# Forming the output projection weight gradients of layers 3 and 2 inside the attention backwards of layers 3 and 1

## The chip, the cores and the metric

The kernel runs on one core of a Trainium2 chip. The core has five engines, each with its own instruction stream: TensorE (PE in the profile; its weight loads have a row of their own, PEld), VectorE (DVE), ScalarE (ACT), GpSimd (POOL) and SyncE (SP), which here issues every DMA transfer from one queue. The metric is the device time of one execution in microseconds; lower is better.

## The reference

Four residual layers with the same shapes, A, B, A, B; layers 0 and 2 share the weights of A, layers 1 and 3 those of B. T = 2048 rows, D = 640, 32 heads of 20. All tensors are bf16. Only the middle of each layer differs:

```
layernorm(x):  (x - mean) / sqrt(var + 1e-5)
A:  qkv = ln @ wqkv;  phi(t) = where(t > 0, t + 1, exp(t)) + 1e-6
    o = phi(q) (phi(k)^T v) / (phi(q) . sum_s phi(k) + 1e-6)      # no mask, whole sequence
B:  qkv = ln @ wqkv
    o = softmax(q k^T * 20**-0.5, where 0 <= i - j < 256) v       # sliding window
x = x + o @ wo                                                    # after each layer
```

The kernel returns the output and, for a given gradient `grad_out`, the gradients of x, A_wqkv, A_wo, B_wqkv and B_wo (`jax.vjp`). The weight gradients are sums over the two layers that share a weight. With `o[l]` the attention output, `g[l]` the gradient behind layer l, `hn[l]` the normalised input and `dqkv[l]` the gradient of qkv,

```
dWo_B = o[3]^T g[3] + o[1]^T g[1]         dWo_A = o[2]^T g[2] + o[0]^T g[0]        (640 x 640)
dW_B  = hn[3]^T dqkv[3] + hn[1]^T dqkv[1] dW_A  = hn[2]^T dqkv[2] + hn[0]^T dqkv[0] (640 x 1920)
```

A change here concerns when these four sums are formed and by which instructions.

## The kernel before, in words

Rows are handled in 16 tiles of 128. `passes` (L1350 onwards) runs the stages one after the other:

1. `forward`, to about 660 us: all four layers; `o`, `hn` and other tensors of each layer go to DRAM.
2. `core(st, 3, ...)`, the attention backward of layer 3, about 664 to 1082 us.
3. The linear backward of layer 2 (`plan_linear`), to about 1259 us.
4. `core(st, 1, ...)`, the attention backward of layer 1, about 1259 to 1666 us.
5. The linear backward of layer 0, in which the products of `weight_jobs` fill the gaps on PE, to about 1968 us.
6. What is left of `weight_jobs`, to the end.

**Order.** For PE, DVE, ACT and GpSimd the instructions run in the order in which this program issues them (`manual_schedule`). The DMA order on SP is chosen by the framework's scheduler. There is one queue on SP; a transfer that has to wait for its data holds everything behind it. The semaphores of the transfers go round in a set of eight, so that each transfer also waits for the one issued eight before it. `PLACES` (L39) holds positions of pieces of work in the visits, found beforehand.

**The core.** `core` (L1288) makes 192 visits and 6 more to drain: 8 chunks of two row tiles, and in each chunk 4 groups of heads (`qr`) of 6 visits. One `core_visit` (L690) works on several visits at a time, with a lag of 3, 4 and 6: it issues the score products `s` and the products `dp`, the exponential `e<-s` on ACT (L719), the product `ds<-dp,e` on DVE (L723), the masks on GpSimd (L734, L738), then the transposes of an older `ds` into a PSUM tile `flip` (L745) with its copy `dsT` (ACT L750, or DVE), a piece of the surrounding row work (`piece`: among it the dense products that share the PSUM pool), and the products `acc` of a still older visit (`core_acc`). Visits 0 to 23 (chunk 0) have tiles of 128 x 512, later ones 128 x 1024. From visit 48 on, the flip of some visits is made by DMA (`by_dma`, L673). The PSUM pool `st.ps` has two buffers under the tag "m", used by `flip`, `dense` and others; `s` and `dp` have one buffer each. The score products read slabs (`slabT`, `slabqT`, `slabqs`, `slabks`) that are loaded a group of six visits ahead.

Ahead of a `flip`, `warm` (L174 to L177) issues `thin` transposes of the identity matrix into unused columns of the same PSUM tile. Nothing reads their result. In visits 0 to 23 of each core there are `WARM[0]` = 8 of them, in 24 to 47 `WARM[1]` = 5, later 0 to 5 by `PLACES["th"]`; visits 0 to 3 have no flip and so none.

`hooks` (filled in `passes`, run in `core` at visit 0.75 k) hold the loads of transposed weights in the first visits of the core of layer 3: `turned` issues a DMA transpose (`WTB`, `WoTA`), and two of the results go back to DRAM (`WTAt`, `WoTBt`).

**The weight products.** `weight_jobs` (L1134) is a generator. It forms the four matrices in the order dWo_B, dW_B, dWo_A, dW_A. For each, blocks of w columns (240 for W, 160 for Wo; 480 and 320 when `W.wide`) and five row blocks m: one chain of 2 x 16 products into one PSUM bank `wg`, over both layers, then one eviction `wr<-wg` (ACT L1211 or DVE L1213) and one store. The left operand `lhs` (one layer's `o` or `hn`, 2.6 MB) comes from pools `wl` (2 buffers), `wl3` (1) and later `wl4` (2); `rhs` from two halves of a big tile, issued at m = 1 of the block before. In the linear backward, `fill(us)` pulls products until a credit is used up: 1.0 a slot after slot 24 of the rest of the core, 0.8 a slot of `plan_linear`; each product counts w/2400. Between the first matrix and the second, while lhs buffers are short (`W.tight`), the generator gives `yield 8.0`, which uses up ten slots. `fill(1e9)` at the end runs all that is left. The output tiles `wr` have 5 buffers in the linear stage and 4 of 480 columns behind it.

```
for n in range(48):
    thin[n] = self.WARM[n // 24]
```

Of the kernel before, what the change touches and what calls it, by code (L numbers as in the profile page):

```python
# [11 lines left out]
ALU = mybir.AluOpType  # L12
# [43 lines left out]
class Kern:  # L56
    def __init__(self, ctx, tc, x0, A_w, A_wo, B_w, B_wo, grad, outs):
# [19 lines left out]
        self.x2 = d("x2", [T, D])  # L77
        self.WTA, self.WoTB = d("WTAt", [P, NF * D]), d("WoTBt", [P, DT * D])
# [598 lines left out]
    WARM = (8, 5)  # L677
    TAIL = 5

# [10 lines left out]
    def core_visit(self, st, l, u, piece, on_act, thin):  # L690
# [443 lines left out]
    def weight_jobs(self, W):  # L1134

        nc = self.nc
        n = 2 * TT
        E = 4

        def lhs(arr):  # L1140
            t = W.lhs.pop(0).tile([P, TT, D], BF, name="lhs")
# [4 lines left out]
        def operand():  # L1146
            W.turn += 1
            if not W.wide:
                return W.big[:, W.turn % 2]
            if W.late is None:  # L1150
                W.late = W.wq2.tile([P, n, 480], BF, name="rhs2")
                W.turn = 1
            if W.turn % 2:
                return W.late
            return W.big.rearrange("p a n w -> p (a n w)").rearrange("p (n w) -> p n w", n=n)

        def rhs(arrs, c0, w):
            t = operand()
            for i, ar in enumerate(arrs):
                for a in range(0, TT, 8):  # L1160
                    self.dma(t[:, i * TT + a:i * TT + a + 8, 0:w], ar[a * P:(a + 8) * P, c0:c0 + w].rearrange("(t p) f -> p t f", p=P))
            return t

        def first(L, R, w):

            ls = [W.lhs.pop(0).tile([P, TT, D], BF, name="lhs") for _ in range(2)]
            r = operand()
            for i in range(2):
                for a in range(0, TT, 8):
                    self.dma(r[:, i * TT + a:i * TT + a + 8, 0:w], R[i][a * P:(a + 8) * P, 0:w].rearrange("(t p) f -> p t f", p=P))  # L1170
                    for b in range(a, a + 8, E):
                        self.dma(ls[i][:, b:b + E, :], L[i][b * P:(b + E) * P, :].rearrange("(t p) f -> p t f", p=P))
            return ls, r
        mats = []
        for kind, layers, names in (("B", (3, 1), ("Wo", "W")), ("A", (2, 0), ("Wo", "W"))):
            for mat in names:
                L, R, out, w, full = ((self.hn, self.dq, self.dW[kind], 240, QT) if mat == "W"
                                      else (self.o, self.gs, self.dWo[kind], 160, D))
                mats.append(([L[k] for k in layers], [R[k] for k in layers], out, w, full))

        def after(i, c0, w):
            c0 += w
            if c0 >= mats[i][4]:
                i, c0 = i + 1, 0
            if i == len(mats):
                return None
            return i, c0, mats[i][3] * (2 if W.wide and c0 + 2 * mats[i][3] <= mats[i][4] else 1)
        job, nxt = (0, 0, mats[0][3]), None
        while job is not None:
            i0, c0, w = job  # L1190
            L, R, out = mats[i0][:3]
            if nxt is None:
                nxt = first(L, R, w)
                yield 0.0
            ls, r = nxt
            for m in range(DT):
                if m == 1:
                    job = after(i0, c0, w)
                    if job is not None:
                        nxt = ls, rhs(mats[job[0]][1], job[1], job[2])  # L1200
                if m == 2 and job is not None and job[1] == 0:
                    L2 = mats[job[0]][0]
                    nxt = [lhs(L2[0]), None if W.tight else lhs(L2[1])], nxt[1]
                ps = W.ps.tile([P, 512], F32, name="wg")
                for i in range(n):
                    self.mm(ps[:, 0:w], ls[i // TT][:, i % TT, m * P:(m + 1) * P], r[:, i, 0:w], i == 0, i == n - 1)
                    if i < n - 1:
                        yield w / 2400.0
                o = W.out()
                if m % 2:  # L1210
# [3 lines left out]
                self.dma(out[m * P:(m + 1) * P, c0:c0 + w], o[:, 0:w])  # L1214
                yield w / 2400.0
            if nxt[0][1] is None:
                nxt[0][1] = lhs(L2[1])
                yield 8.0
# [69 lines left out]
    def core(self, st, l, g_out, B, hooks):  # L1288
# [17 lines left out]
        thin = [PLACES["th"][n % 24] for n in range(nv)]  # L1306
        for n in range(48):
            thin[n] = self.WARM[n // 24]
        on_act = [PLACES["xx"][n % 24] for n in range(nv)]
        n = 0  # L1310
        with ExitStack() as es:
# [3 lines left out]
            for c in range(NC):  # L1315
                for qr in range(4):
                    S = B.slabs.pop(0)
                    for i, u in enumerate(self.core_visits(st, l, S, c, qr, dq)):
# [12 lines left out]
                        self.core_visit(st, l, u, slots[n], on_act[n], thin[n])  # L1331
# [18 lines left out]
    def passes(self):  # L1350
# [6 lines left out]
        with ExitStack() as rest:  # L1357
# [17 lines left out]
            left3 = self.core(st, 3, self.gs[2], st.core, hooks)  # L1375
# [170 lines left out]
```

## Time and profile before

| what | value |
|---|---|
| time, median of 3 runs | 2187.86 us (2182.36 to 2193.05) |
| profiled execution: span, first to last instruction | 2185.5 us; no time beside the span is given for it |
| PE busy (matmul) | 2023.2 us, 93% |
| PE weight loads | 1564.4 us, 72% |
| DVE / ACT / GpSimd busy | 1338.7 / 1364.0 / 1040.7 us |
| mean granted clock of PE | 0.970 |
| identity transposes of L177 into `flip` | 764 |
| weight products `wg<-rhs,lhs` | 2880: 640 x 160 wide, 1280 x 240, 320 x 320, 640 x 480 |
| DMA | 426.92 MB, 708455 packets, mean 195 GB/s |

The visits of the two cores, by the start of their exponential: layer 3 visit 0 at 664.2, visit 10 at 683.3, visit 24 at 708.5, visit 48 at 759.6; layer 1 visit 0 at 1259.5, visit 4 at 1267.1, visit 24 at 1299.6, visit 48 at 1350.0.

How to read the profile: busy times of engines overlap, so they say where time could go and not what bounds it. The row PEclk tells what clock PE was granted, in tenths of full speed, in 40 slices of the span. A group line names the source line (L142 is the helper that issues every product), the engine, the operation and what it writes and reads. A bracket such as [4.69 <-DMA slabqT<-T] behind an instruction is the idle time of its engine before it, and what ended it.

### The profile page before, as it was taken

To read this page: it belongs to the slowest core of one execution; us is meant where nothing else is said; L and a number is where in the kernel's file an instruction comes from. 1 tells how busy PE (TensorE), PEld (TensorE's weight loads), DVE (VectorE), ACT (ScalarE), POOL (GpSimd) and SP (SyncE) were. 2 spreads that over 40 slices of the span, in tenths; PEclk is the share of its full clock that TensorE was granted. 3 is DMA by queue.
4 is the path that set the end of the run, shared out by engine and by line. 5 is a ranking of instruction groups with operands and counts; after the bars stand their busy time and mean duration, and the time that the engine had idled before them with its cause. 6 is when DMAs were issued, how large, how long until landed. Compare 5 with 4: busy or idle time off the path is not lost. (4 is left out here: it accounts for less than half of the span.)

```text
span 2185.5 us, 76656 instructions
## 1 busy us (share of the span) xinstructions
PE 2023.2 (93%) x32575; PEld 1564.4 (72%) x32575; DVE 1338.7 (61%) x2710; ACT 1364.0 (62%) x1907; POOL 1040.7 (48%) x1663
## 2 busy tenths in 40 slices
PE   7989998899988999999979989999998999999999
PEld 5667776577766877777758768777776888888644
DVE  6788886888844777777738747777776233320000
ACT  5468886388876888888737679888886133330000
POOL 2046665166665577777533456777764212220000
PEclk9999999999998999999889999999999999999999
DMA  7498985689888299998889922899998899988650
GB/s 258 149 224 225 227 206 145 158 218 209 226 223 211 69 177 188 188 188 176 164 263 255 234 82 74 185 196 188 187 196 186 265 309 241 276 202 252 210 163 21
DMA packets 708455, 426.92 MB, mean 195 GB/s; under 512 B 434320, under 2 KB 689040, under 8 KB 707728
## 3 DMA queue, kind: packets, MB, share of 16 engines
q1 hardware_dynamic: 708112, 422.03, 78.7%
q8 instruction: 254, 4.16, 0.8%
q14 instruction: 89, 0.73, 0.1%
HBM read 191.07 MB, written 141.43 MB: 152 GB/s over the span
## 5 line engine op out<-in xcount | busy, mean ns | idle before, releaser
L723 DVE TENSOR_TENSOR ds<-dp,e 128x1024 bf16<-128x1024 f32 (+1 forms) x384 | 443.9, 1156 | 166.0 <-PE s L142 80.5
L719 ACT ACTIVATE e<-s 128x1024 bf16<-128x1024 f32 (+1 forms) x384 | 380.1, 990 | 90.4 <-PE s L142 85.9
L387 ACT ACTIVATE eT<-sT 128x2048 bf16<-128x2048 f32 x180 | 338.0, 1878 | 96.5 <-PE sT L142 88.5
L142 PE MATMUL wg<-rhs,lhs 128*128 128x240 bf16 (+3 forms) x2880 | 374.2, 287 | 7.7 <-DMA lhs<-o 6.8
L142 PEld LDWEIGHTS <-lhs 128*128 128x128 bf16 x2880 | 262.6, 99 | 98.9 <-DMA lhs<-o 8.4
L738 POOL TENSOR_SCALAR_AFFINE_SELECT e<-e 128x256 bf16<-128x256 bf16 x512 | 201.6, 409 | 174.4 <-ACT e L719 143.8
L142 PEld LDWEIGHTS <-dqT 128*128 128x128 bf16 x1920 | 169.9, 98 | 66.7 <-issue 9.1
L395 POOL TENSOR_SCALAR_AFFINE_SELECT eT<-eT 128x512 bf16<-128x512 bf16 x256 | 164.7, 647 | 102.3 <-ACT eT L387 102.3
L750 ACT COPY dsT<-flip 128x1024 bf16<-128x1024 bf16 (+1 forms) x200 | 192.2, 961 | 12.4 <-PE flip L745 11.2
L142 PE MATMUL acc<-slabqs,ds 128*128 128x20 bf16 x2880 | 194.3, 172 | 0.6 <-ACT dq L805 0.5
L142 PE MATMUL acc<-ds,e 128*128 128x20 bf16 x2880 | 192.2, 171 | 0.0
L142 PE MATMUL dp<-slabT,dT 32*128 32x128 bf16 (+1 forms) x1952 | 154.1, 246 | 38.4 <-DVE ds L723 32.1
L142 PEld LDWEIGHTS <-ds 128*128 128x128 bf16 x2880 | 176.1, 96 | 10.9 <-issue 6.8
L1211 ACT CAST wr<-wg 128x240 bf16<-128x240 f32 (+3 forms) x36 | 14.3, 396 | 249.8 <-PE wg L142 249.8
L734 POOL TENSOR_SCALAR_AFFINE_SELECT e<-e 128x512 bf16<-128x512 bf16 x224 | 142.7, 637 | 55.6 <-ACT e L719 53.2
L142 PEld LDWEIGHTS <-e 128*128 128x128 bf16 x2880 | 164.1, 96 | 5.7 <-issue 0.5
L1213 DVE CAST wr<-wg 128x240 bf16<-128x240 f32 (+3 forms) x54 | 24.5, 453 | 231.3 <-PE wg L142 231.3
L142 PE MATMUL dense<-WTA,dqT 128*128 128x320 bf16 x960 | 163.5, 302 | 2.0 <-DMA dqT<-dqa 1.7
L1106 POOL TENSOR_TENSOR dh<-dh,lg 128x640 f32<-128x640 f32 x32 | 46.0, 1439 | 245.4 <-DVE s L1103 245.4
L142 PE MATMUL dense<-WB,hnT 128*128 128x320 bf16 x960 | 162.0, 303 | 0.4 <-DVE s L510 0.2
L142 PE MATMUL s<-slabT,slabqT 32*128 32x128 bf16 (+1 forms) x1952 | 148.4, 247 | 10.7 <-ACT e L719 5.2
L142 PE MATMUL dense<-WTB,dqT 128*128 128x320 bf16 x960 | 156.1, 301 | 1.1 <-DMA dqT<-dq 0.7
(175 smaller groups left out, 4445.4 us busy)
## 6 DMA issues: line engine op xcount, KB each, us to landing
T<-T SPq DMA_DIRECT2D x96, 256.0 KB, 3.3
s<-s SPq DMA_DIRECT2D x32, 512.0 KB, 3.7
slabT<-T SPq DMA_DIRECT2D x64, 256.0 KB, 3.9
dqkv<-dq SPq DMA_DIRECT2D x16, 960.0 KB, 5.9
dqkv<-dqa SPq DMA_DIRECT2D x32, 480.0 KB, 4.9
rhs<-dqkv SPq DMA_DIRECT2D x32, 480.0 KB, 5.9
rhs<-dqkv SPq DMA_DIRECT2D x16, 960.0 KB, 7.1
hn<-hn SPq DMA_DIRECT2D x64, 160.0 KB, 2.7
```

Of the source, the lines that this page charges most:

```text
L142: return self.nc.tensor.matmul(out, lhsT=lhsT, rhs=rhs, start=start, stop=stop, skip_group_check=True, **kw)
L387: nc.scalar.activation(e, s, ACT.Exp)
L395: nc.gpsimd.affine_select(out=e, in_=e, compare_op=ALU.is_ge, fill=0.0, base=0, pattern=[[0, 4], [1, P]], channel_multiplier=-1)
L719: nc.scalar.activation(u.e[:, :, 0:w], s[:, :, 0:w], ACT.Exp)
L723: nc.vector.tensor_tensor(out=d.ds[:, :, 0:w], in0=d.dp[:, :, 0:w], in1=d.e[:, :, 0:w], op=ALU.mult)
L734: nc.gpsimd.affine_select(out=v, in_=v, pattern=[[0, 4], [1 if far else -1, P]], **kw)
L738: nc.gpsimd.affine_select(out=v, in_=v, pattern=[[0, 2], [1 if far else -1, P]], **kw)
L750: nc.scalar.copy(v(f.dsT), v(ps))
L1106: nc.gpsimd.tensor_tensor(out=x["dh"], in0=x["dh"], in1=L["g"][:, i, :], op=ALU.add)
L1211: nc.scalar.copy(o[:, 0:w], ps[:, 0:w])
L1213: nc.vector.tensor_copy(o[:, 0:w], ps[:, 0:w])
```

## The change

Three parts belong together.

- **Early blocks.** `early_weights` forms o[3]^T g[3] in the core of layer 3, and o[2]^T g[2] in the core of layer 1, as 25 blocks of 128 x 128 each: 16 products 128 wide in a PSUM tile of tag "m" (`wgp`), one copy to an f32 tile by DVE, one store of 64 KB into a new DRAM tensor (`pw`). The left operand is 8 loads of 320 KB (`wgl`) into buffers of the pool `st.sp` that are used for other tiles later; the right operand is five column blocks of 512 KB (`wgr`, rows of 256 bytes), loaded two ahead. A block runs in `core_visit` ahead of the flip, in visits 10 to 46 of layer 3 (10 + 38i//25) and 4 to 46 of layer 1 (4 + 44i//25). In layer 3 the loads begin in `hooks[10]`, visit 7; in layer 1 ahead of the core.
- **Idle transposes.** From the first block on, `thin` is 0 in visits below 48, with or without a block. Those that stay are in visits 4 to 9 of layer 3 (8 each) and beyond visit 48. The whole kernel has 252 in place of 764.
- **The weight products.** `weight_jobs` is rewritten. The order is dW_B (both layers), dWo_B (layer 1 alone), dW_A (both), dWo_A (layer 0 alone). The Wo blocks are 320 wide with chains of 16, and DVE adds the partial sum, loaded back as f32 (`pt`, 3 buffers), while it evicts. The products are 2400: 1600 x 240, 320 x 320 and 480 x 480 (dW_A goes in blocks of 240, 480, 480, 480 and 240 columns); the pools of `lhs` shrink (no `wl4`), the output tiles are 2 of 320 columns in the linear stage, and the rest of `yield 8.0` is gone: while a left operand has no buffer, the generator gives `yield 1.0`.

On SP the change adds 84 transfers (1375 to 1459). In the core of layer 3 the scheduler now puts `wgr` and the eight `wgl` behind the third transpose of `WTB` from A, ahead of the next `slabqT`; the three transposes of `WTB` from B, one queue entry behind each other before, now come one by one behind the slabs of chunk 1; the load of `gb` and `WoTA` come later too. In layer 2's linear backward the eight `wgl` of the core of layer 1 are issued near its start. The rhs of the first block of `weight_jobs` goes ahead of all its lhs.

The diff, without the removed lines of `weight_jobs` (they stand above):

```diff
+        self.pw = {(k, nm): d(f"p{nm}{k}", [P, DT * w], F32) for k in "AB" for nm, w in (("Wo", D), ("W", QT))}
...
-    WARM = (8, 5)
+    WARM = 8
     TAIL = 5
+
+    def early_weights(self, st, la, dst):
+
+        w = 128
+        L, R = [], {}
+
+        def left():
+            for i, tag in enumerate(("hnb", "gc", "oa", "pqb", "gn", "gn", "dn", "dn")):
+                t = st.sp.tile([P, 2, D], BF, name="wgl", tag=tag, bufs=2 if i > 3 else 1)
+                self.dma(t, self.pair(self.o[la], i))
+                L.append(t)
+
+        def right(c):
+            R[c] = st.sp.tile([P, TT, w], BF, name="wgr", tag="dqT", bufs=3)
+            self.dma(R[c], self.gs[la][:, c * w:(c + 1) * w].rearrange("(t p) f -> p t f", p=P))
+
+        def block(c, m):
+            ps = st.ps.tile([P, 512], F32, name="wgp", tag="m")
+            for k in range(TT):
+                self.mm(ps[:, 0:w], L[k // 2][:, k % 2, m * P:(m + 1) * P], R[c][:, k, :], k == 0, k == TT - 1)
+            o = st.sf.tile([P, D], F32, name="wgo", tag="f")
+            self.nc.vector.tensor_copy(o[:, 0:w], ps[:, 0:w])
+            self.dma(dst[:, m * D + c * w:m * D + (c + 1) * w], o[:, 0:w])
+            if m == 0 and c + 2 < D // w:
+                right(c + 2)
+        return left, right, [lambda c=c, m=m: block(c, m) for c in range(D // w) for m in range(DT)]
...
+        if extra is not None:
+            extra()
         if f is not None and not f.by_dma:
...
         E = 4
...
+        def lhs(arr, pool):
+            t = pool.tile([P, TT, D], BF, name="lhs")
             for a in range(0, TT, E):
                 self.dma(t[:, a:a + E, :], arr[a * P:(a + E) * P, :].rearrange("(t p) f -> p t f", p=P))
             return t
...
+        def operand(n, w):
             W.turn += 1
...
+            if W.wide and W.late is None:
+                W.late = W.wq2.tile([P, 2 * TT * 480], BF, name="rhs2")
+                W.turn = 0
+            t = W.big[:, W.turn % 2] if not W.wide else W.big.rearrange("p a n -> p (a n)") if W.turn % 2 else W.late
+            return t[:, 0:n * w].rearrange("p (n w) -> p n w", n=n)
         def rhs(arrs, c0, w):
...
+            t = operand(len(arrs) * TT, w)
             for i, ar in enumerate(arrs):
                 for a in range(0, TT, 8):
...
+                    self.dma(t[:, i * TT + a:i * TT + a + 8, :], ar[a * P:(a + 8) * P, c0:c0 + w].rearrange("(t p) f -> p t f", p=P))
             return t
...
+        def sums():
+            for m in mats:
+                for c0 in range(0, D, 320):
+                    for j in range(DT):
+                        if m["mode"] == "add":
+                            yield part(m, c0, j, 320)
+        def part(m, c0, j, w):
+            t = W.out.tile([P, 320], F32, name="pt", bufs=3)
+            self.dma(t, m["part"][:, j * D + c0:j * D + c0 + w])
+            return t
+        def mat(mode, kind, nm, layers, c0=0, c1=None):
+            R, out, full = (self.dq, self.dW, QT) if nm == "W" else (self.gs, self.dWo, D)
+            return dict(mode=mode, L=[(nm, k) for k in layers], R=[R[k] for k in layers], out=out[kind], full=full, c0=c0, c1=c1 or full,
+                        part=self.pw[kind, nm], ls=[])
+        mats = [mat("all", "B", "W", (3, 1)), mat("add", "B", "Wo", (1,)), mat("all", "A", "W", (2, 0)), mat("add", "A", "Wo", (0,))]
+        want, at = [], {}
+        def pump():
+            while want and (W.lhs or want[0][1] in at):
+                m, arr = want.pop(0)
+                if arr not in at:
+                    at[arr] = lhs((self.hn if arr[0] == "W" else self.o)[arr[1]], W.lhs.pop(0))
+                m["ls"].append(at[arr])
+        def ask(i):
+            if i < len(mats):
+                want.extend((mats[i], k) for k in mats[i]["L"])
+                pump()
+        def blocks():
+            for i, m in enumerate(mats):
+                c0 = m["c0"]
+                while c0 < m["c1"]:
+                    w = 320 if len(m["R"]) == 1 else 240
+                    if W.wide and len(m["R"]) > 1 and c0 + 2 * w <= m["c1"]:
+                        w *= 2
+                    yield i, m, c0, w
+                    c0 += w
+        todo = blocks()
+        more, pt = sums(), []
+        i, m, c0, w = next(todo)
+        r = rhs(m["R"], c0, w)
+        nxt = (None, None, 0, 0)
+        ask(0)
+        yield 0.0
+        while m is not None:
+            pump()
+            while len(m["ls"]) < len(m["L"]):
+                yield 1.0
+                pump()
+            if c0 == m["c0"]:
+                for k in [k for k in at if k not in m["L"]]:
+                    del at[k]
+                ask(i + 1)
+            n = len(m["R"]) * TT
+            for j in range(DT):
+                pump()
+                if j == 1:
+                    nxt = next(todo, (None, None, 0, 0))
+                    if nxt[1] is not None:
+                        r2 = rhs(nxt[1]["R"], nxt[2], nxt[3])
+                if m["mode"] == "add" or nxt[1] is not None and nxt[1]["mode"] == "add" and j > 2:
+                    pt.append(next(more, None))
+                add = pt.pop(0) if m["mode"] == "add" else None
                 ps = W.ps.tile([P, 512], F32, name="wg")
...
+                for k in range(n):
+                    self.mm(ps[:, 0:w], m["ls"][k // TT][:, k % TT, j * P:(j + 1) * P], r[:, k, :], k == 0, k == n - 1)
+                    if k < n - 1:
                         yield w / 2400.0
...
+                o = W.out.tile([P, W.most], BF, name="wr")
+                if add is not None:
+                    nc.vector.tensor_tensor(out=o[:, 0:w], in0=ps[:, 0:w], in1=add, op=ALU.add)
+                elif j % 2:
                     nc.scalar.copy(o[:, 0:w], ps[:, 0:w])
                 else:
                     nc.vector.tensor_copy(o[:, 0:w], ps[:, 0:w])
...
+                self.dma(m["out"][j * P:(j + 1) * P, c0:c0 + w], o[:, 0:w])
                 yield w / 2400.0
...
+            (i, m, c0, w), r = nxt, r2
...
-            thin[n] = self.WARM[n // 24]
+            thin[n] = self.WARM if n < min(extra) else 0
...
+            work = {}
+
+            def begin_early(la, kind):
+                work["left"], work["right"], work["blocks"] = self.early_weights(st, la, self.pw[kind, "Wo"])
+                work["right"](0)
+                work["left"]()
+                work["right"](1)
+            h8 = hooks[10]
+            hooks[10] = lambda: (h8(), begin_early(3, "B"))
+            left3 = self.core(st, 3, self.gs[2], st.core, hooks, [(10 + i * 38 // 25, lambda i=i: work["blocks"][i]()) for i in range(25)])
...
+            begin_early(2, "A")
+            left1 = self.core(st, 1, self.gs[0], B, [f or (lambda: None) for f in hooks], [(4 + i * 44 // 25, lambda i=i: work["blocks"][i]()) for i in range(25)])
...
-            W.big, W.turn, W.wide, W.late = self.pool(rest, "wq", 1).tile([P, 2, 2 * TT, 240], BF, name="rhs"), 0, False, None
-            wo = self.pool(rest, "wo", 5)
+            W.big, W.turn, W.wide, W.late = self.pool(rest, "wq", 1).tile([P, 2, TT * 480], BF, name="rhs"), 0, False, None
+            W.out, W.most = self.pool(rest, "wo", 2), 320
             st.ex = self.pool(psl, "ex", 1)
-            W.lhs, W.tight = [wl, wl], True
-            W.out = lambda: wo.tile([P, 240], BF, name="wr")
+            W.lhs = [wl, wl]
...
-            wl4 = self.pool(rest, "wl", 2)
-            W.lhs += [wl4, wl4, wl, wl3]
-            W.tight, W.wide = False, True
-            W.wq2, wo2 = self.pool(rest, "wq2", 1), self.pool(rest, "wo2", 4)
-            W.out = lambda: wo2.tile([P, 480], BF, name="wr")
+            W.lhs += [wl, wl3]
+            W.wide, W.wq2 = True, self.pool(rest, "wq2", 1)
+            W.out, W.most = self.pool(rest, "wo2", 4), 480
             fill(1e9)
```

More of the change, by code (lines that the diff above doesn't have):

```diff
@@ L1174, in weight_jobs @@
[L1174 to L1203, printed above, removed]
+        def sums():
[4 more added lines that the diff above has]
+                            yield part(m, c0, j, 320)
@@ L1286, in core_loads, with core @@
         return S
-    def core(self, st, l, g_out, B, hooks):
+    def core(self, st, l, g_out, B, hooks, early):
         NC = TT // 2
@@ L1330, in core @@
                             dq[c] = dqp.tile([P, 2, QT], BF, name="dq")
-                        self.core_visit(st, l, u, slots[n], on_act[n], thin[n])
+                        self.core_visit(st, l, u, slots[n], on_act[n], thin[n], extra.get(n))
                         n += 1
@@ L1418, in passes @@
             self.core_buffers(st, B)
-            left1 = self.core(st, 1, self.gs[0], B, [f or (lambda: None) for f in hooks])
+            begin_early(2, "A")
+            left1 = self.core(st, 1, self.gs[0], B, [f or (lambda: None) for f in hooks], [(4 + i * 44 // 25, lambda i=i: work["blocks"][i]()) for i in range(25)])
             for f in left1[:8]:
```

36 lines of the change are left out of this document (2 added, 34 removed).

## The prediction, made before the changed kernel had run

> **What bounds the kernel now.** I read the page first: engine shares, the clock row, the shares of the chain that ended last. Then busy time by stretch, cut where the stages change (attention backward of layer 3 from 664, linear backward of layer 2, attention backward of layer 1 from 1259.5, then linear backward of layer 0 with the weight products, and from 1968.4 weight products alone). Then the instructions of TensorE (PE) and SyncE's queue (SP) in time where the edit falls.
>
> ```profile
> PEclk9999999999998999999889999999999999999999
> PE 21%; DMA 2%; SPq 1%; DVE 1%; ACT 0%; issue 0%; DVEq 0%; ACTq 0%
> ```
>
> ```profile
> 708.50:759.60 51.10, 48.76 (x1109) 41.76 (x1110) 37.35 (x48) 44.66 (x62) 29.68 (x58) 0.97 0.26 77
> ...
> 1259.50:1299.60 40.10, 36.33 (x676) 29.93 (x676) 19.02 (x32) 28.36 (x56) 23.50 (x46) 0.87 0.28 82
> 1299.60:1350.00 50.40, 47.81 (x1103) 40.64 (x1101) 36.82 (x48) 44.58 (x63) 29.66 (x58) 1.00 0.20 59
> ...
> 1968.40:2185.00 216.60, 210.87 (x1297) 127.40 (x1294) 14.58 (x28) 9.16 (x19) 2.94 (x2) 0.98 0.52 163
> ```
>
> Columns: stretch, length, busy time of PE, weight loads, VectorE (DVE), ScalarE (ACT), GpSimd, then granted clock, DMA share, GB/s. In the first 48 visits of both cores PE is the busiest engine, ACT a little behind; PE's "busy" includes idle transposes. The last 217 us are PE alone.
>
> ```profile
> 1287.90 0.62 PE L177 MATMUL flip<-ident 128*128 128x128 bf16 x8
> 1288.36 0.39 PE L745 MATMUL flip<-ident,ds 128*128 128x128 bf16 x4
> ```
>
> ```profile
> 1726.22 8.46 PE L142 MATMUL wg<-rhs,lhs 128*128 128x160 bf16 x120
> ```
>
> ```profile
> 2044.05 0.49 DVE L1213 CAST wr<-wg 128x320 bf16<-128x320 f32 x1 [8.20 <-PE wg L142]
> ...
> 2052.68 0.49 DVE L1213 CAST wr<-wg 128x320 bf16<-128x320 f32 x1 [8.14 <-PE wg L142]
> ```
>
> Eight idle transposes take 1288.36 − 1287.90 = 0.46 us until the next starts, 56 ns each. A 160-wide weight product takes 8.46/120 = 70 ns. Evictions of 320-wide chains come 8.63 us apart on DVE for two chains (ACT has the other): 4.32 each, 135 ns per product.
>
> **Part 1, the end.** Removed: layer 3's and 2's Wo products. Before, Wo B was 640 products 160 wide: 640 × 0.0695 = 44.5. Wo A was 320 products 320 wide: 43.5. After, layers 1 and 0 alone, 320 products 320 wide: 43.5 for both. The 240- and 480-wide products of W keep their volume (A W regrouped from 129.6 to 130.0). Sum −44.1, all on PE's path, which is 150.0 of 150 busy from 1800 to 1950 and 97% at the end. The fill credit is per product width, so fewer products in the fill zone only draw later ones forward.
>
> Moved with it: the first matrix is now W of B. Its rhs is issued ahead of all lhs, and layer 1's o (2.6 MB) ahead of linear 0's first loads.
>
> ```profile
> 1781.04 0.90 PE L1009 MATMUL flip<-ident,dqa 128*128 128x128 bf16 x5 [3.55 <-DVE dqa L1056]
> ...
> 2006.56 0.72 PE L142 MATMUL wg<-rhs,lhs 128*128 128x320 bf16 x4 [0.99 <-DMA lhs<-o]
> ```
>
> At 1770–1787 the old generator rested (its `yield 8.0`); PE was idle 3.55 and then at half clock, which cost about 3.4 more: −7, if filled. Against it, the earlier o loads: before, the first `ldn` was issued at 1742.5 and its flip ran at 1751.3, with a landing of 4.1, so 4.6 of slack; 2.6 MB at 308 GB/s is 8.5 us: +3.5 (bounds 0 and 8.5). The first chain waits for all of the rhs: +1.5 (0 to 4). The stall before the third matrix (3.0 idle on `lhs<-o` and its half clock, 6.3 in all) stays, as a wait for `lhs<-hn`: 5 to 9, +0.5. Output buffers: two instead of five while linear 0 runs. Chains of 2.2 to 4.4 us and out stores landing in 1.7 to 4.4 just fit, but a store queued behind a load holds a buffer, its evicting engine and two chains later PE: 0 to 5, I take 1. Adding `pt` on DVE replaces a copy of 0.49; its 160 KB loads run one ahead in the queue. Together −7 + 3.5 + 1.5 + 0.5 + 1 = −0.5: **−44** (−52 to −34).
>
> **Part 2, the first 48 visits.** Added: 2 × 25 blocks of 16 products, 128 wide: 800. Removed: 764 − 252 = 512 idle transposes. Nearest row for a block product is that of the transposes, the same shape at 56 ns (160 wide: 70, which would be 56 us for 800; I take 56 ns, same width and a weight load per product). Balance 800 × 0.056 − 512 × 0.056 = **+16.1**. From below: the four stretches of the 48 visits hold 2.3 to 7.3 us of PE idle each, 16.1 in all, of which 4.7 is the stall at 702.97 counted below; if all 11.3 left were filled, +5. From above: 196 of the removed transposes stand in visits without a block, and if those visits gain nothing, because ACT sets them, 11.0 is not given back: +27, less 2.9 of idle in block visits: +24. In the first 24 visits PE is full (20.08 of 20.20 at 1279–1300), so there the removal pays; in the second 24 ACT has 44.6 of 50.4, so part is lost. I take **+17** (5 to 26).
>
> ACT and GpSimd get nothing new here. DVE gets 50 copies of 128×128, under 0.32 (the 160-wide cast), at 73% of load: hidden, unless the visit's next user of the two PSUM buffers ("m", shared with `flip` and `dense`) waits for one queued behind `ds` (L723, 1.16 mean); in front of the block stands that `ds`, issued about a block's 0.9 earlier, so the copy is due when the block ends. 0, with up to 50 × 0.1 kept in the upper end.
>
> **Part 3, the queue.** SP is one queue, and its order changes in core 3.
>
> ```profile
> 675.60 0.53 SPq L109 DMA_DIRECT2D slabqT<-T  x1
> ...
> 692.06 12.07 SPq L109 DMA_TRANSPOSE WTB<-in_B_wqkv_dram  x3
> ...
> 704.80 0.47 SPq L109 DMA_DIRECT2D slabqT<-T  x1
> ```
>
> ```profile
> 702.97 0.23 PE L142 MATMUL dp<-slabT,dT 32*128 32x128 bf16 x2
> 707.88 0.39 PE L142 MATMUL s<-slabT,slabqT 32*128 32x256 bf16 x2 [4.69 <-DMA slabqT<-T]
> ```
>
> Visit 24's `slabqT` was issued behind three weight transposes (12.07 us of queue) and PE stood 4.69, then ran at half clock for about 0.9 loss. After, those transposes come behind this load: −5.6. New: from 675.6 the queue issues a `wgr` and eight `wgl` and a second `wgr` (about 3.1 MB until block 0 is fed). At 305 to 336 GB/s, the most that stretches of this trace moved, that is 9.3 to 10 us plus landing, so 686 to 689, and the block of visit 10 is due at 683.3: a stall of 3.5 (2 to 8), half clock behind it 1.5. Everything behind the block on PE waits too, and all engines with it. Visit 12's `slabqT` is behind these loads also (needed at about 686.5), in the shadow of the same stall. Net **−0.5**.
>
> The stores of blocks (64 KB) wait on SP for the copy by DVE, and the slab loads queue behind them; the stores follow each other by 1.3 to 4 us, a group of six visits lasts 8 to 13. Cost 0 here; see the second rival. Core 1: its eight `wgl` (2.6 MB, 8 us of bandwidth) are queued at the start of linear layer 2, a stage that moves 243 GB/s at 0.88 DMA share and where PE is busy 157 of 174: +1 (0 to 4). Its visits from 1261 to 1271 run at half clock (0.52), where blocks 4 and 5 cost double: +1.
>
> **Sum.** −44 + 17 − 0.5 + 2 = −25.5. Against the profiled span of 2185.5, which lies 2.4 under the median of the three runs (no other time of that execution is given), this is −1.2%; on the median **2162 us**. About 0.5%, 11 us, is what a measurement of this kernel can tell from no change; the runs spread over 10.7.
>
> **Rivals.**
> *Block products are dearer.* At the 160-wide price of 70 ns and with nothing from visits without a block: 56 − 28.7 + 11 = 38 instead of 17, so 2183. For it: a block needs a new weight tile per product and PSUM shared with `flip`. Against: idle transposes load weights as often and take 56. The Trainium skill, "TensorE: Matmul & The Clock Gate", Back-to-back issue gap, says that streams of weight load and product settle at about 81 ns for 128 columns and calls the 56 an isolated figure. By that page 800 would cost 64.8, 20 more than here, and the time would be 2182; the trace's transposes at 56 ns and 160-wide products at 70 speak against it. Chance 0.07.
>
> *Slower: stores hold the slabs.* A store waits at the head of SP for a block that PE does late; the next group's `slabqT` or `slabqs` stands behind, PE waits for it, which delays the next block. One such stall is the one at 702.97: 4.7 and 0.9. There are 16 groups in the two cores' first 48 visits. From 25.5/5.6, 5 of them, nothing is left; with 8, +19: 2207. Against: but for the stalled one, `slabqT` was issued 9 to 17 us before the visit that uses it. Chance 0.08.
>
> *The clock falls without idle transposes.* Where clock was 0.52 (1261–1271) a visit took 1.93 for 1.50. 32 visits lose all their transposes and get no block: 32 × 0.43 = 14, so 2176; all 82 affected: 35, 2197. Against: each such visit stands next to a block, and from 759.6 on, with 0 to 5 transposes, the clock is 0.97. Chance 0.05.
>
> *The end gives back half.* Loads or the two output buffers hold PE for some 20 us at the matrix changes (three, each 6 to 7 as at 2006): 2182. Against: DMA moved 163 GB/s at the end. Chance 0.07.
>
> **The numbers.** Forecast 0.73, its own range 2150 to 2176 from the bounds of the parts. Its low end with the end at −52 and the visits at +10 is 2146; the high end takes in the first and last rival, to 2184; what is left out is the second rival, the worst of the third and tails, 0.18. Faster: 0.73 and the mild ends of the last two, 0.76; same: 0.14; slower: 0.10.
>
> **What would show it.** Right: rows of `flip<-ident` fall from 764 to 252; `wgp` has 800 products at 56 ns spacing; the wait for `slabqT` at 703 is gone and one for `wgl` stands at visit 10; visits 4 to 48 of core 1 take 91 us instead of 82.9; after linear 0's last dense product 166 us remain instead of 217. Wrong: waits on `slabqT`/`slabqs` in the 48 visits, a clock under 0.9 there, blocks spaced 70 ns or more, or waits of `wg` on `lhs` and `wr` over 10 us in all.

## The result and the profile after

The changed kernel takes 2165.7 us (median of 4 runs, 2158.86 to 2171.06) against 2186.85 us before (4 runs): a ratio of 0.9897, 95% interval 0.9868 to 0.9925. The forecast was 2162 with a range of 2146 to 2184. A second set of runs of the same kernel gave 2165.7 again, ratio 0.9898 (0.9878 to 0.9918). The profiled execution took 2162.49 us, its span is 2160.8. (In the traces SyncE issues 1464 transfers before and 1535 after, 71 more and not 84.)

From the starts of the exponential `e<-s` (first visit, visits 24 and 48, last visit of each core) both traces can be cut into the same stages, so that the difference of the two spans falls into place:

| stage, us | before | after | difference |
|---|---|---|---|
| to visit 0 of layer 3 | 664.2 | 662.3 | −1.9 |
| layer 3, visits 0 to 23 | 44.3 | 51.6 | +7.3 |
| layer 3, visits 24 to 47 | 51.0 | 57.4 | +6.3 |
| layer 3, visit 48 to the last | 322.0 | 320.0 | −2.0 |
| last visit of layer 3 to visit 0 of layer 1 | 177.9 | 175.7 | −2.3 |
| layer 1, visits 0 to 23 | 40.1 | 44.6 | +4.4 |
| layer 1, visits 24 to 47 | 50.3 | 55.7 | +5.3 |
| layer 1, visit 48 to the last | 316.3 | 318.0 | +1.7 |
| from there to the end | 519.2 | 475.6 | −43.6 |
| span | 2185.5 | 2160.8 | −24.7 |

The change does two things and each is visible by itself: the end is 43.6 us shorter, the four stretches of early visits together are 23.4 longer. Stages in which no instruction changed (from visit 48 on) differ by 2 us here and by up to 9 over all traces below (314 to 324 for layer 1); the four runs of the changed kernel lie 12 us apart.

The next lines are busy times by stretch of the changed kernel (columns as in the prediction: stretch, length, PE, weight loads, DVE, ACT, GpSimd, each with its number of instructions, then granted clock, DMA share, GB/s):

```profile
662.30:713.90 51.60, 43.06 (x734) 34.10 (x735) 23.58 (x46) 28.34 (x55) 20.67 (x43) 0.87 0.87 237
713.90:771.30 57.40, 54.59 (x1224) 47.08 (x1224) 39.79 (x63) 45.94 (x63) 29.70 (x58) 1.00 0.64 148
...
1267.00:1311.50 44.50, 39.01 (x703) 32.55 (x703) 22.30 (x44) 27.98 (x56) 23.51 (x46) 0.86 0.56 147
1311.50:1367.20 55.70, 51.16 (x1191) 44.62 (x1191) 39.15 (x61) 45.59 (x62) 29.63 (x58) 1.00 0.29 83
...
1994.50:2160.80 166.30, 157.04 (x980) 96.30 (x978) 14.34 (x28) 5.71 (x11) 2.94 (x2) 0.98 0.52 160
```

The granted clock of the early visits is what it was (0.86 and 1.00 in layer 1, where it was 0.87 and 1.00; 0.87 and 1.00 in layer 3, where the kernel before has 0.88 and 0.97). The last row begins 1.7 us behind the last dense product of linear layer 0, which ends at 1992.8: from there 168 us of weight products alone remain, where it was 217.

The groups by line and form of the changed kernel (busy, mean ns of one, idle before them):

```profile
L143 PE MATMUL wgp<-wgr,wgl 128*128 128x128 bf16 x800 | 57.4, 226 | 5.8 <-DMA wgl<-o 5.3 <-DVE ds L871 0.2
...
L178 PE MATMUL flip<-ident 128*128 128x128 bf16 x252 | 32.7, 225 | 3.1 <-ACT dsT L779 2.6 <-DVE ds L871 0.4
```

And one visit of it in time on PE:

```profile
1302.41 1.07 PE L143 MATMUL wgp<-wgr,wgl 128*128 128x128 bf16 x16
1303.32 0.39 PE L774 MATMUL flip<-ident,ds 128*128 128x128 bf16 x4
```

A block holds PE for 1303.32 − 1302.41 = 0.91 us, 57 ns per product. (The mean of 226 ns in the group line is not the spacing: the products overlap, and all 16 together are counted as 1.07 us.)

What PE waited for in the first visits of layer 3, and the first block itself:

```profile
682.07 0.28 PE L143 MATMUL wgp<-wgr,wgl 128*128 128x128 bf16 x2 [0.59 <-DMA wgl<-o]
684.26 0.28 PE L143 MATMUL wgp<-wgr,wgl 128*128 128x128 bf16 x2 [1.91 <-DMA wgl<-o]
685.15 0.28 PE L143 MATMUL wgp<-wgr,wgl 128*128 128x128 bf16 x2 [0.60 <-DMA wgl<-o]
...
690.21 1.89 PE L143 MATMUL wgp<-wgr,wgl 128*128 128x128 bf16 x16
```

The first block takes the eight loads of its left operand one after the other as they land, over 7.8 us in place of 0.9; the second runs at half clock (1.89 us; granted clock 0.50 from 689.0 to 692.3). The wait of 4.69 for `slabqT` at visit 24 is gone: from the score products of visit 23 to those of visit 24 it is 1.7 us, where it was 6.2.

At the end, the waits of PE from visit 191 of layer 1 on, before:

```profile
PE wg L142 <- DMA lhs<-o: 6.8, 5, 2.3
PE flip L1009 <- DVE dqa L1056: 3.5, 1, 3.5
```

and after:

```profile
PE wg L143 <- DMA lhs<-hn: 9.4, 6, 4.3
PE flip L167 <- DMA ldn<-dn: 4.3, 1, 4.3
```

Columns are us in all, times, longest. The waits for `lhs` stand in two places: before the first matrix they were 3.9 and are 3.3, before the third they were 3.0 and are 6.2, now for layer 0's hn instead of o. The wait for `dqa` went with the pause of the generator, as forecast, but in its place stands one of 4.3 for linear 0's first loads (`ldn`), which are issued behind the lhs of layer 1's o. Together PE waits for about 20 us in this stage, where it was 17.

### The profile page after: what moved, and what is told of

Read it like the earlier page. It is cut to its first block, busy times and chain, and to the rows that moved or that the text cites. A ratio compares the mean times of both kernels' runs of the same rounds, so it can differ in the third digit from the quotient of the medians.

```text
span 2160.8 us, 76514 instructions
## 1 busy us (share of the span) xinstructions
PE 1987.2 (92%) x32383; PEld 1545.5 (72%) x32383; DVE 1352.8 (63%) x2765; ACT 1361.9 (63%) x1897; POOL 1040.9 (48%) x1663
## 5 line engine op out<-in xcount | busy, mean ns | idle before, releaser
L143 PE MATMUL wg<-rhs,lhs 128*128 128x240 bf16 (+2 forms) x2400 | 332.6, 293 | 9.6 <-DMA lhs<-hn 9.4
L143 PEld LDWEIGHTS <-lhs 128*128 128x128 bf16 x2400 | 231.7, 99 | 85.4 <-DMA lhs<-hn 11.8
L396 POOL TENSOR_SCALAR_AFFINE_SELECT eT<-eT 128x512 bf16<-128x512 bf16 x256 | 164.7, 647 | 100.3 <-ACT eT L388 100.3
L399 POOL TENSOR_SCALAR_AFFINE_SELECT eT<-eT 128x512 bf16<-128x512 bf16 x224 | 143.3, 640 | 18.1 <-ACT eT L388 17.7
L774 PE MATMUL flip<-ident,ds 128*128 128x128 bf16 x1824 | 147.7, 223 | 4.1 <-DVE ds L871 3.9
```

What stands on the lines that cost most here:

```text
L143: return self.nc.tensor.matmul(out, lhsT=lhsT, rhs=rhs, start=start, stop=stop, skip_group_check=True, **kw)
L396: nc.gpsimd.affine_select(out=e, in_=e, compare_op=ALU.is_ge, fill=0.0, base=0, pattern=[[0, 4], [1, P]], channel_multiplier=-1)
L399: nc.gpsimd.affine_select(out=e, in_=e, compare_op=ALU.is_ge, fill=0.0, base=-1, pattern=[[0, 4], [-1, P]], channel_multiplier=1)
L774: nc.tensor.transpose(ps[:, 4 * j + i, :], f.ds[:, j, i * P:(i + 1) * P], self.ident)
```

## Experiments

**The end alone.** Blocks taken out, idle transposes put back, weight products of the changed kernel. The partial sums come from zeros written in the core of layer 3.

```diff
-            hooks[10] = lambda: (h8(), begin_early(3, "B"))
+            def zeros():
+                for k in "AB":
+                    for j in range(DT):
+                        o = st.sf.tile([P, D], F32, name="wgo", tag="f")
+                        self.nc.gpsimd.memset(o, 0.0)
+                        self.dma(self.pw[k, "Wo"][:, j * D:(j + 1) * D], o)
+            hooks[10] = lambda: (h8(), zeros())
...
-            thin[n] = self.WARM if n < min(extra) else 0
+            thin[n] = (8, 5)[n // 24]
```

> The end of the change alone: no early blocks, the 512 idle transposes back as before, the new weight products kept; the partial sums that they add are zeros, so that the Wo gradients of layers 3 and 2 are left out. If the parts add up, the end gives its 44 us whole and the visits cost nothing: about 2143. If half of the end's gain was owed to the changed visits, or is given back to waits: about 2165.

2155.4 us (ratio 0.9855, 0.9829 to 0.988): neither the one nor the other. By stages the end was 473.7, so 45.5 shorter, but visits 0 to 23 of layer 3 took 61.5 in place of 44.3. The fault was in the experiment:

```profile
PE dp L143 <- DVE ds L750: 19.3, 3, 18.1
```

```profile
684.62 0.63 POOL L1439 MEMSET wgo<- 128x640 f32 x1 [2.82 <-DMA pWoA<-wgo]
...
693.82 2.17 POOL L1439 MEMSET wgo<- 128x640 f32 x3 [5.81 <-DMA pWoA<-wgo]
```

The first line is a wait of PE in the visits, the others GpSimd in time. The memsets waited for buffers that were held by stores, the masks of the visits stood behind the memsets on GpSimd, `ds` behind the masks, PE behind `ds`. So it was run again with one memset at visit 46.

```diff
+                o = st.sf.tile([P, D], F32, name="wgo", tag="f")
+                self.nc.gpsimd.memset(o, 0.0)
+                for k in "AB":
+                    for j in range(DT):
+                        self.dma(self.pw[k, "Wo"][:, j * D:(j + 1) * D], o)
+            hooks[62] = zeros
```

> As the run of the end alone, Wo gradients of layers 3 and 2 left out, but the zeros come from one tile that is set once, in visit 46 of layer 3, so that nothing waits for GpSimd in visit 10 (18.1 us there in the first form). The stage behind the core of layer 1 again at 473 to 476 us; the whole 2141 to 2145. If the sum of parts does not hold even so, 2150 or more.

2145.1 us, ratio 0.9789 (0.9762 to 0.9817), which is 45.5 under the runs of before beside it; the last stage 473.2. The end's gain stands by itself and is whole.

**The blocks alone.** The kernel before, with `early_weights`, the blocks and the thinner `thin` of the change, and its own weight products.

```diff
+        extra = dict(early)
         for n in range(48):
-            thin[n] = self.WARM[n // 24]
+            thin[n] = 8 if n < min(extra) else 0
...
+        if extra is not None:
+            extra()
         if f is not None and not f.by_dma:
```

> The kernel before with the early blocks and without the 512 idle transposes, the weight products as before; the partial sums are stored and read by nothing. If the parts add up, this shows the price of the visits: 23 us by the two traces (13.6 in the core of layer 3, 9.7 in that of layer 1), 2210. By the prediction's own sum (17 - 0.5 + 2) 2205. At 70 ns and more per product it would be 2220 and above.

2205.4 us, ratio 1.0081 (1.0058 to 1.0103): 18.5 slower. The prediction's own sum for parts 2 and 3 (17 − 0.5 + 2) is 18.5. The four stretches are 207.4 in place of 185.7, so 21.7 by the trace. With the end alone the two add up to −45.5 + 18.5 = −27, against −21 measured for both together. Each of the three is known to about 5 or 6, so whether anything stands behind these 6 us stays open.

**The idle transposes alone.** The kernel before, without the 512 transposes.

```diff
-            thin[n] = self.WARM[n // 24]
+            thin[n] = 8 if l == 3 and n < 10 else 0
```

> The kernel before without the 512 idle transposes that the change removes, and nothing else. Theory: they are work on PE's path in the first 24 visits and lie beside ACT in the second 24: up to 34 x 0.45 = 15 us faster, I expect 10, 2177, with the granted clock of the visits unchanged. Rival (they hold the clock): the clock of the two cores' first visits falls below 0.8 and the time stays or rises, to 2200 if all 34 visits take 1.93 instead of 1.50.

2181.8 us (12 runs), ratio 0.9973 (0.9956 to 0.999): 5 us (2 to 10) of the 10 expected. The four stretches are 183.7 in place of 185.7, although 28.7 us of PE's work is gone, and the stall ahead of visit 24 is 3.1 shorter in this execution (1.6 for 4.7), so that the visits themselves gained nothing. The stretches, first one of the kernel before (layer 3, visits 0 to 23), then the four without the transposes:

```profile
664.00:708.50 44.50, 37.18 (x687) 29.84 (x683) 20.80 (x37) 28.53 (x55) 20.80 (x44) 0.88 1.01 234
...
666.80:707.70 40.90, 34.52 (x571) 26.58 (x572) 20.30 (x37) 28.36 (x55) 20.56 (x43) 0.76 1.02 232
707.70:759.60 51.90, 45.95 (x988) 37.16 (x989) 36.66 (x48) 44.52 (x62) 29.53 (x58) 0.89 0.33 93
1255.40:1294.40 39.00, 33.93 (x512) 25.36 (x512) 18.53 (x32) 28.13 (x57) 23.38 (x46) 0.62 0.29 83
1294.40:1346.30 51.90, 45.69 (x984) 36.92 (x984) 36.45 (x48) 44.72 (x63) 29.53 (x58) 0.90 0.21 59
```

The granted clock fell in all four: 0.76, 0.89, 0.62 and 0.90, where the kernel before has 0.88, 0.97, 0.87 and 1.00. The mean clock of the whole kernel fell in every run (0.958 to 0.965 in the 12, 0.967 to 0.976 in the 22 beside them). But the clock is the smaller part of the answer. Visit by visit (by the starts of their score products, visits 10 to 47 of layer 3 and 4 to 47 of layer 1), 48 visits had the full clock in both traces: they lost 276 transposes, 15.5 us of PE, and became 1.8 us shorter. In 24 that fell to half clock, the products that are left took longer, and these visits became 4 us longer. So most of the removed work had lain in time in which PE would otherwise have waited: in visits 24 to 47 of layer 1 its idle time went from 2.6 us (47.81 busy of 50.40) to 6.2 (45.69 of 51.90). My expectation that the clock would not change was wrong. The prediction's reading that in the first 24 visits, where PE is counted full, the removal pays, held for less than a third: 12 of them with the full clock in both traces lost 5.4 us of transposes and became 1.6 us shorter. The rival was right about the clock of visits 0 to 23 (below 0.8) and about visits that do not get shorter; that they would be 14 longer was too much.

**The idle transposes kept beside the blocks.**

```diff
-            thin[n] = self.WARM if n < min(extra) else 0
+            thin[n] = (8, 5)[n // 24]
```

> The changed kernel with all idle transposes of before kept beside the blocks (8 in visits below 24, 5 in 24 to 47). Theory: 512 x 0.056 = 28.7 us of PE time, less what fits in the idle of about 20 visits of 24 to 47 without a block (5.6): 21 to 23 us slower than the changed kernel, 2188. Rival (the clock gains from them): the same as the changed kernel or faster, 2160 to 2166.

2181.9 us (12 runs), 16.2 over the changed kernel, less than the 21 to 23 expected; the four stretches 228.3 in place of 209.3, so 19. The clock is about as with the blocks alone: 0.90 and 1.00 in layer 1, and in layer 3 0.85 and 1.00:

```profile
662.80:719.90 57.10, 49.63 (x850) 40.68 (x851) 24.08 (x47) 28.44 (x55) 20.69 (x43) 0.85 0.87 230
719.90:781.50 61.60, 59.20 (x1341) 52.69 (x1339) 40.16 (x63) 45.78 (x62) 29.66 (x58) 1.00 0.53 124
```

Once the blocks are there, the transposes do next to nothing for the clock and cost PE time. So the same 512 instructions are worth 5 us where nothing takes their place and 16 where blocks do. Where the difference lies is seen in visits 24 to 47 of layer 1, in which the granted clock is 1.00 in all three of these traces (us, by the starts of the score products):

| | 13 visits with a block in the change | 11 without |
|---|---|---|
| transposes alone (before) | 24.8 | 25.4 |
| blocks alone (the changed kernel) | 31.2 | 24.4 |
| both (this run) | 34.3 | 24.8 |

Beside a block the 65 transposes cost 3.1 of their 3.6 us, in visits without one the 55 cost 0.4 to 1.0 of 3.1. So a transpose has nearly its full price beside a block, and a third of it or less elsewhere, at the same clock. On this the price of the visits rests: 23.4 us instead of 228.3 − 185.7 = 42.6 with the transposes kept.

**The first block later.** Blocks of layer 3 in visits 16 to 46, loads where they were.

```diff
-..., [(10 + i * 38 // 25, lambda i=i: work["blocks"][i]()) for i in range(25)])
+..., [(16 + i * 32 // 25, lambda i=i: work["blocks"][i]()) for i in range(25)])
```

> The changed kernel with the 25 blocks of layer 3 in visits 16 to 46 instead of 10 to 46; loads as before, idle transposes stay in visits 10 to 15. Theory: the wait for the left operand at visit 10 and the half clock behind it (8.6 us by the trace) go, 48 transposes more cost 2.7: 6 faster than the changed kernel, 2160. Rival (the first block is late wherever it stands, or the wait passes to a slab): no change, 2166.

2167.2 us, ratio 0.9899 (0.9872 to 0.9926): nothing gained. The wait for `wgl` was gone and another stood in its place, at visit 12:

```profile
691.90 0.28 PE L143 MATMUL s<-slabT,slabqT 32*128 32x128 bf16 x2 [7.46 <-DMA slabqT<-T]
```

```profile
675.81 6.46 SPq L110 DMA_DIRECT2D wgl<-o  x8
682.31 0.71 SPq L110 DMA_DIRECT2D wgr<-in_grad_out_dram  x1
683.12 6.50 SPq L110 DMA_DIRECT2D slabqT<-T  x1
```

The slab is issued behind the 3.1 MB, and its issue itself takes 6.50. The stall belongs to the queue, not to the block.

**The slab ahead of the loads.** Loads begun at visit 8 instead of 7, blocks in visits 14 to 46.

```diff
-            h8 = hooks[10]
-            hooks[10] = lambda: (h8(), begin_early(3, "B"))
+            h8 = hooks[11]
+            hooks[11] = lambda: (h8(), begin_early(3, "B"))
-..., [(10 + i * 38 // 25, ...
+..., [(14 + i * 34 // 25, ...
```

> The changed kernel with the loads of layer 3's blocks begun one visit later (visit 8), so that the slab of visits 12 to 17 is queued ahead of them, and the blocks in visits 14 to 46. Theory: what PE waits for around visit 10 to 12 is the 3.1 MB in one queue ahead of whatever comes next, so the wait goes only where both the slab and the first block have time: the 7.5 to 8.6 us go, four visits with 8 idle transposes more cost 1.8: 6 faster than the changed kernel. Rival (a stall of that size returns elsewhere, at the slab of visit 18 or the first block): the same as the changed kernel.

In the trace visits 0 to 23 of layer 3 take 46.8 in place of 51.6, and the wait for `wgl` is 0.7 in all. But visits 24 to 47, where the blocks stand closer now, take 1.6 more (59.0 for 57.4), and of the 6 us little is left: 2163.5 us, ratio 0.9894 (0.9872 to 0.9916), not to be told from the changed kernel beside it:

> The changed kernel itself, unedited, to have it on the same chip as the three others: 0.990 of the kernel before, about 2166.

(2165.7 us, 0.9898.)

**Layer 0's hn earlier.** Its buffer is given to the weight products as soon as dW_B is done.

```diff
-                W.lhs += [wl3, wl]
+                W.lhs += [wl3, wl, wl]
...
-            W.lhs += [wl, wl3]
+            W.lhs += [wl3]
```

> The changed kernel with the buffer for layer 0's hn given to the weight products as soon as dW_B is done, so that its four loads are queued some 30 us earlier. Theory: the wait before dW_A (6.2 us idle at 1999 to 2007 and about 1 to 2 of half clock) goes: 7 faster, 2159. Rival: the stage moves 252 GB/s at 0.91 DMA share, so 2.6 MB more in it makes linear 0 late by as much: 2166.

2162.6 us, ratio 0.9883 (0.9857 to 0.9908); the stage itself 477.4, not shorter than 475.6. The rival was right about that stage. The waits of PE there:

```profile
PE dense L143 <- DMA dqT<-dqa: 6.4, 1, 6.4
...
PE wg L143 <- DMA rhs<-dqkv: 3.3, 3, 1.2
...
PE wg L143 <- DMA lhs<-hn: 2.0, 2, 1.1
```

The 6.2 us of waiting before the third matrix became 6.4 for a transpose that linear 0 needs, queued behind eight loads, and 3.3 for `rhs`. The 2.0 for `lhs` are those before the first matrix, 3.3 in the changed kernel. Together with the later first block it gave no more:

> Both edits together (blocks of layer 3 from visit 16, layer 0's hn loaded early). The two lie in different stages, so the gains add: 13 faster than the changed kernel, 2153. If one of the two passes its wait on, 2159.

2169.3 us, 0.9906 (0.9882 to 0.993): both waits had moved, none had gone.

**Layer 0's hn 14 slots before the end of linear 0**, behind its last store of `dqkv` and ahead of the first `rhs` of dW_A.

```diff
...
+                    if q == len(every) - 14:
+                        W.lhs += [wl]
...
-            W.lhs += [wl, wl3]
+            W.lhs += [wl3]
```

> The changed kernel with layer 0's hn loaded 14 slots before the end of linear layer 0, behind its last stores of dqkv and ahead of the first rhs of dW_A, not 30 us early and not behind the last store of out. Theory: then neither the last transposes of linear 0 (6.4 us late when the loads were early) nor dW_A (6.2 us late) wait: 5 faster than the changed kernel, 2161. Rival (2.6 MB more at 0.91 DMA share must be waited for somewhere): the same.

The stage is 471.8, 3.8 shorter. The 2.7 us for `lhs<-hn` that are left stand before the first matrix; before the third PE now waits for an output buffer instead:

```profile
PE wg L143 <- DVE wr L1262: 5.1, 2, 4.6
...
PE wg L143 <- DMA lhs<-hn: 2.7, 3, 1.1
```

In whole times, 2165.4 us and 0.9892 (0.9865 to 0.9918), it does not show.

> Both edits: 11 faster than the changed kernel, 2155, if each holds; else what the two alone show, summed.

With the slab ahead as well: 2159.7 us, ratio 0.9871 (0.9847 to 0.9894). That is 6.0 under the changed kernel on the same chip and the fastest of the kernels here that leave nothing out; in the trace visits 0 to 23 of layer 3 and the last stage, the two that the edits aim at, are 46.5 and 472.8 instead of 51.7 and 475.8. But visits 24 to 47 of layer 3 take 61.2 instead of 57.4 there, and the traced execution as a whole (span 2163.2) is longer than that of the changed kernel beside it (2159.0), so the traces do not show the 6.0. The intervals of the two ratios overlap, so that this kernel beats the one before for certain and the changed one only probably.

## Why the prediction was right, step by step

- **Part 1, −44.** Measured −43.6 between the traces and −45.5 alone. The removed products at 69.5 and 135 ns are the main term, −44.1, and it held: the products that are left follow each other at the same spacing as before. (With the small terms, −0.5, the forecast's own sum is −44.6 and not −44.) After linear 0's last dense product 168 us remain, where 166 were forecast. The small terms add up about as forecast, near nothing, but not one by one. The pause (3.5 idle, then half clock from 1780.1 to 1787.0) and the late `ldn` (4.3 idle, half clock from 1771.1 to 1777.9) cost about the same, so that filling the one and opening the other gave nothing, where −7 + 3.5 was forecast: the half clock around the second wait was left out. PE's idle time before the third matrix grew by 3.2 (6.2 for 3.0), where +0.5 was forecast. Before the first matrix it shrank, where +1.5 was forecast, and some 2 us more of the gain are not accounted for. That these offset each other is luck. The two output buffers cost PE nothing in the changed kernel (it has no wait for `wr` in this stage); they showed only when another wait was taken away.
- **Part 2, +17.** The blocks alone, with part 3, cost 18.5 by the times, where 18.5 was forecast, but 21.7 by the trace of that run and 23.4 by the two traces of the change. As part 3 alone was 3.6 dearer than forecast, the exact agreement is luck; and the span of the changed kernel came out within 1 us of the forecast because four stages that the change hardly touches were 4.5 us shorter in this pair of traces. The 56 ns per product was right (57). Visits 4 to 48 of layer 1 take 92.6 us (91.7 in the second set), where 91 was forecast. The reasoning behind the upper bound was right too: by the starts of their score products, the 11 visits of 24 to 47 of layer 1 without a block took 24.4 us for 25.4, so that of their 55 transposes (3.1 us) only a third came back. The 50 copies on DVE (0.29 each) were hidden but for 1.2 us in which PE waits for one. The +1 for linear layer 2 is not seen: 175.7 for 177.9, and 173 to 178 over the traces.
- **Part 3, −0.5.** Both signs were right, one size was not. The 5.6 at visit 24 came back. The stall at visit 10 was put at 5.0; visits 10 to 13 of the changed kernel take 15.9, and with the loads out of the way they take 5.9 (the slab-first run), with three blocks in place of transposes 5.9 + 3 × 0.45 = 7.3: the stall cost 8.6. The last load was there at 688.8, as forecast (686 to 689), but PE came to the block at 681.2 and not at 683.3, since the changed kernel's trace is 2 us ahead there, and so block 10 took 6.9 us more than its 0.9. At half clock block 11 took 1.7 instead of 0.9. The slab of visit 12, issued behind these loads, cost nothing here: PE does not wait for it. These 3.6 us are as much as the forecast missed the median by, though the scatter of single runs is larger.
- **Dearer products** (70 to 81 ns): excluded by the spacing of 57 ns. The 81 ns of the Trainium skill ("TensorE: Matmul & The Clock Gate", Back-to-back issue gap) do not hold for this stream, in which each block is 16 pairs of weight load and product.
- **Stores hold the slabs:** no wait for a slab appears in the 48 visits of the changed kernel. No run shows a store that holds a slab. Two runs show its parts: a slab late by 7.46 us behind loads in this queue, and PE held for 18.1 us because stores kept the buffers of GpSimd's memsets.
- **The clock falls:** it did not (0.86 to 1.00 with blocks, 0.62 to 0.90 without transposes and without blocks). Of the two arguments against it, that each such visit stands next to a block was the right one: the blocks hold the clock in the transposes' stead. The other (0.97 from 759.6 on with few transposes) did not bear on it. The price of 1.93 for 1.50 is found at visit 25 of layer 3 (709.8 to 711.7, at half clock) beside visit 25 of layer 1, not at 1261 to 1271 as said. And a clock under 0.9 was no sign of being wrong: the changed kernel has 0.87 and 0.86 in visits 0 to 23, but the kernel before has 0.88 and 0.87.
- **The end gives back half:** it did not, by the −45.5 of the end alone.

## What to carry to other kernels

In this kernel, idle instructions that keep an engine's clock up cost little to keep and gained little when they were dropped (5 us of 28.7), mostly because they lay where the engine would have waited anyway. They cost more than half of their time (16 us) once useful work stood beside them. Moved work is then priced by the balance on that engine (products in, transposes out, at the spacing read from the trace), and removed work at a stage that is one engine alone by products times spacing. On one queue, a load put earlier moves the wait to whatever was behind it: two of four such edits changed the name of the wait and not the time. The other two made their own stage 3 to 5 us shorter, by a place in the queue where what stands behind had slack, but in whole times neither can be told from the changed kernel.

## What was not expected of the hardware

With eight identity transposes per visit the granted clock was 0.87 over visits 0 to 23 of layer 1; without them it was 0.62 while PE was still counted busy for 33.9 of 39.0 us. The Trainium skill ("TensorE: Matmul & The Clock Gate", Part 4: PE-mode transpose) says that transposes do not count as PE activity in the same way as products; these runs show that they hold the clock all the same, and the measurement decides. Whether one of them counts as much as a product, no run here shows. Nor are PE's gaps enough to explain the low clock: without the transposes there is a stretch of 13.7 us at half clock in which PE is counted busy for 13.59 and in which the profile shows no wait of PE:

```profile
1278.40:1292.10 13.70, 13.59 (x235) 11.38 (x230) 7.52 (x13) 12.00 (x24) 5.33 (x14) 0.50 0.08 22
```

The kernel before has the full clock there (1.00 from 1271.5 to 1292.1, with 20.12 of 20.60 us busy). What keeps the clock down in this stretch stays open.
